# A fused attention and gMLP kernel: another recorded order for four compute engines, and a narrower marking product

## The chip, the cores and the metric

The kernel runs on one core of one Trainium2 chip. A core has five engines that run their own instruction streams in order: TensorE (PE, matrix products), VectorE (DVE), ScalarE (ACT), GpSimd (POOL) and SyncE (SP, which here only issues transfers). [...] The metric is device time in microseconds (us), the median over runs; smaller is better.

## What is computed

The input x has 2048 tokens of 512 numbers, in bf16. A linear attention block with 32 heads and a residual is followed by a gMLP mixer with a residual:

```
def _A_ref(x, wqkv, wo):
    qkv = (x @ wqkv).reshape(B, S, 3, H, Dh)        # H = 32, Dh = 16
    phi = lambda t: where(t > 0, t + 1, exp(t)) + 1e-06
    pq, pk = phi(q), phi(k)
    kv = einsum('bhsd,bhse->bhde', pk, v)
    z = einsum('bhsd->bhd', pk)
    num = einsum('bhqd,bhde->bhqe', pq, kv)
    den = einsum('bhqd,bhd->bhq', pq, z)[..., None] + 1e-06
    return (num / den).transpose(0, 2, 1, 3).reshape(B, S, D) @ wo

def _B_ref(x, w_in, w_sp, b_sp, w_out):
    z = gelu(einsum('bsd,df->bsf', x, w_in))        # F = 1792
    z1 = z[..., :Fh]                                # Fh = 896
    z2 = layernorm(z[..., Fh:])
    g = einsum('ts,bsf->btf', w_sp, z2) + b_sp[None, :, None]
    return einsum('bsf,fd->bsd', z1 * g, w_out)

h = x + _A_ref(layernorm(x), A_wqkv, A_wo)
h2 = h + _B_ref(layernorm(h), B_w_in, B_w_sp, B_b_sp, B_w_out)
```

## The kernel before

**How the order is set.** The kernel does not issue instructions as its code is read. Each step is recorded in a list by `_Prog.add` (an engine, a function that issues the instructions, the memory it reads and writes), and the dependencies are found from the overlap of the footprints: pieces of on-chip memory, and whole banks of the accumulator memory (psum, 8 banks of 512 floats per partition). `schedule` (L144) then decodes the string `ORDER` (L16), a compressed list of the numbers of all 1315 recorded steps in the order in which they are to be issued; each engine gets its own part of it, in that order. `emit` (L163) puts a semaphore wait before each step whose input comes from another engine. The string and the record together fix all five streams: 349 steps on PE, 456 on VectorE, 255 on ACT, 129 on GpSimd and 126 on SP. A step may issue several instructions (eight matmuls, say).

Since an engine runs in order, a step that waits holds up all that stands behind it on its engine. An order can therefore change which engine waits for which, and for how long, without a change of what is computed.

**The stages, in time.**

1. *Head and K stage (0 to 46 us).* `k_unit` (L648) takes the tokens in 16 tiles of 128. VectorE computes the statistics of a tile (L543, L544); `norm` (L588, on VectorE or ACT) writes the normalised tile xn; it is turned round, for the first four tiles by PE (`pe_transposes`, L602), for the others by a transposing transfer on SP (recorded through `dma_t`, L467), into xnT. PE multiplies with the K part of wqkv (all products of the helper `matmuls` show up as L434). `phi` (L609) has ACT write exp into e (all of ACT's work through its helper shows up as L453), VectorE clamp it (L614) and combine it into pk (L617, L619). PE adds pk and xn up into four banks over all tiles (L692). A few of the Q products (`q_unit`, L698) are between these. In the same stretch VectorE forms sums of weights (`comb`, L755, into ws and sae) for the block scheme described below.
2. *Small products and h tiles (46 to 73 us).* Context, wv and wo are folded into one matrix m (L790, L801). Denominators (L824) go through ACT (r, rcp) and are spread over partitions by transfers on SP (`spread`, L815, writes r16; the trace names it r); VectorE multiplies them into pqT (L840). For each of 16 token tiles PE forms pqT × m in one of the banks 4, 5 and 7 in turn, VectorE adds x and writes h (L852, which frees the bank), ACT squares it, GpSimd makes mean and variance of it, VectorE normalises (hn, L588), and SP turns it round into hnT.
3. *First mixer stage (66 to 108 us).* z = gelu(hn × w_in). For pairs of tiles, `cell3` (L905) and `cell2` (L922) use a scheme with 7 block products in place of 8, whose input sums are formed on VectorE (hs, ws) and whose outputs are combined by copies of ACT and additions of VectorE within the banks (`add_on`, L882). ACT applies gelu into z2 or z1. z2 is normalised: VectorE or ACT statistics (L952, L953), GpSimd, VectorE (L588).
4. *Spatial product (104 to 212 us).* `mix` (L1067) forms w_sp × z2 for pairs of row tiles in the same 7-product manner (sums wt, sa, zt on VectorE), some of it nested once more (`nested`, L1042, with nu, nv, np). The gate multiplies with z1 (L1030, L1031), SP turns the result round into zgT.
5. *Output (from 175 us, between the steps of 4).* `mo_pair` (L1159) multiplies zgT with w_out for two tiles, again with 7 block products (us, vs sums on VectorE; tmp reads L1176; h written at L1188), and SP stores h.

**The marking product.** A bank of which only a part has been written by a product gets a product of no use into its rest, before later products accumulate onto parts of it. Before, bank 7 gets a 512-column product that starts anew (L1210); bank 4, used by the last pair, gets one over the rest of the bank, 64 columns from HW = 448 to 512 (L1217). Neither contributes to the output.

Of the kernel before, what the change touches and what calls it, by code (L numbers as in the profile page):

```python
# [32 lines left out]
class _Prog:  # L33
# [219 lines left out]
def bass_sequential_preLN__linear_attn_block__mixer_gmlp__prompt_kernel(  # L253
# [11 lines left out]
    _, S, D = A_x.shape  # L265
    F = B_w_in.shape[1]
    FH = F // 2
    H = 32
# [9 lines left out]
    g = _Prog(nc)  # L278
# [43 lines left out]
    x = g.sbuf("x", o_x, [NT, D], BF16)  # L322
    h = g.sbuf("h", o_x, [NT, D], BF16)
# [6 lines left out]
    hnT = g.sbuf("hnT", o_pk, [KD, S], BF16)  # L330
# [4 lines left out]
    z1 = [g.sbuf(f"z1t{n}", o_xnT + slot[n] * ZR, [FH], BF16) for n in range(NT)]  # L335
# [14 lines left out]
    N4 = HT // 2 * (HW // 2) * 2  # L350
# [65 lines left out]
    def bank(b, n=512, lo=0):  # L416
        return psum[:, b, lo:lo + n]
# [5 lines left out]
    def PE(fn, reads, writes, ns, **k):  # L423
        return g.add("PE", fn, reads, writes, cost=ns, lat=165, **k)
# [372 lines left out]
    for c in range(KD):  # L797
        b = CB[1 - c % 2]
# [18 lines left out]
    for tg in range(NG):  # L817
# [12 lines left out]
        if tg not in MERGE:  # L830
# [135 lines left out]
    lo, hi = slice(0, HW), slice(HW, FH)  # L966
# [227 lines left out]
    for k in range(0, HT, 2):  # L1194
# [5 lines left out]
        if k == 0:  # L1200
# [6 lines left out]
                quarter_sums(nv1, z2[:, 0:HT, lo])  # L1207
            if any(m & 2 for m in NEST):
                quarter_sums(nv5, zt1)
    PE(lambda pe: pe.matmul(bank(7), lhsT=hnT[:, 0, 0:P], rhs=wout[:, 0, :], start=True, stop=True), [hnT[:, 0, 0:P], wout[:, 0, :]],  # L1210
       [bank(7)], 216)
    wout_sums()
    for c, i in enumerate(MIX[:-1]):
        X, Y = (3, 4) if i == MIX[-2] else (6, 7)
        if Y != 7:
            rest, any_, w = psum[:, Y, HW:512], zgT[MIX[0]][:, 0, :], wout[:, 0, 0:512 - HW]
            PE(lambda pe, rest=rest, any_=any_, w=w: pe.matmul(rest, lhsT=any_, rhs=w, start=False, stop=True,  # L1217
                                                               skip_group_check=True), [any_, w], [rest], 65)
        mo_pair(i, c % 2, X, Y)
# [34 lines left out]
```

## Time and profile before

| | before |
|---|---|
| runs | 224.6, 223.45, 224.06 us |
| median | 224.06 us |
| span of the profiled execution (first to last instruction) | 222.3 us |
| median less that span | 1.76 us |
| granted TensorE clock, mean | 1.000 |
| busy: PE, VectorE, ACT, GpSimd | 97%, 91%, 64%, 21% of the span |
| moved by transfers | 27.12 MB, mean 122 GB/s |

The profiled execution is told by its span; no whole time is listed for it. In rows of the timeline the columns are start, duration, engine, line, operation, output <- inputs, shape and count; a bracket at the end is the idle time just before, and what released the engine. Matmuls overlap, so that a row's duration is longer than its share of the time: the distance from the start of one row to the start of the next is what counts. Rows by stage give, after the stretch and its length, the busy time (and count) of PE, PE's weight loads, VectorE, ACT and GpSimd, the granted clock, the share of the transfer engines, and GB/s; a row for one engine has that engine alone. In a group of instructions the last columns are total busy time, mean ns of one, and idle time before them.

### The profile page before, as it was taken

To read this page: it belongs to the slowest core of one execution; us is meant where nothing else is said; L and a number is where in the kernel's file an instruction comes from. 1 tells how busy PE (TensorE), PEld (TensorE's weight loads), DVE (VectorE), ACT (ScalarE), POOL (GpSimd) and SP (SyncE) were. 2 spreads that over 40 slices of the span, in tenths; PEclk is the share of its full clock that TensorE was granted. 3 is DMA by queue.
4 is the path that set the end of the run, shared out by engine and by line. 5 is a ranking of instruction groups with operands and counts; after the bars stand their busy time and mean duration, and the time that the engine had idled before them with its cause. 6 is when DMAs were issued, how large, how long until landed. Compare 5 with 4: busy or idle time off the path is not lost.

```text
span 222.3 us, 3865 instructions
## 1 busy us (share of the span) xinstructions
PE 216.2 (97%) x1346; PEld 123.6 (56%) x1346; DVE 202.8 (91%) x472; ACT 142.8 (64%) x283; POOL 47.1 (21%) x133
## 2 busy tenths in 40 slices
PE   7799999999999999999999999999999999999995
PEld 7443444443344444444555556666676787767764
DVE  3899967899999999999989998999999989899995
ACT  5789663299889999999872546626475246732330
POOL 4334410000547554685720000000000000000000
PEclk9999999999999999999999999999999999999999
DMA  6758877928966555304993653995372205033574
GB/s 182 246 99 227 170 180 181 237 50 193 182 137 132 112 107 85 49 0 94 179 134 88 166 116 81 161 202 107 58 152 58 41 0 70 17 88 27 127 203 142
DMA packets 75026, 27.12 MB, mean 122 GB/s; under 512 B 64768, under 2 KB 75008, under 8 KB 75008
## 3 DMA queue, kind: packets, MB, share of 16 engines
q1 hardware_dynamic: 74304, 26.30, 57.0%
q10 hardware_dynamic: 704, 0.59, 0.9%
q8 instruction: 10, 0.16, 0.3%
q14 instruction: 8, 0.07, 0.1%
HBM read 6.95 MB, written 2.10 MB: 41 GB/s over the span
## 4 chain that ended last, share of the span: by engine, by line
PE 87%; DVE 4%; DMA 3%; ACT 3%; SPq 1%; issue 1%; ACTq 0%
PE psum L434 79%; PE psum L692 6%; DMA x<-in_A_x_dram 1%; SPq L815 1%; DMA r<-rcp 1%; ACT e L453 1%; DVE pqT L840 1%; DVE h L852 1%; DVE st L543 1%; DVE pk L619 1%; PE psum L602 0%; PE psum L824 0%; PE psum L714 0%; PE psum L790 0%; DVE e L614 0%
## 5 line engine op out<-in xcount | busy, mean ns | idle before, releaser
L453 ACT ACTIVATE psum<-psum 128x448 f32<-128x448 f32 (+2 forms) x76 | 31.1, 428 | 34.9 <-PE psum L434 28.6
L434 PE MATMUL psum<-z,wt 128*128 128x448 bf16 (+1 forms) x216 | 42.0, 335 | 0.1
L434 PEld LDWEIGHTS psum<-z,wt 128*128 128x128 bf16 x216 | 20.9, 98 | 14.6 <-ACT np L453 0.4
L434 PE MATMUL psum<-win,hnT 128*128 128x448 bf16 x112 | 26.4, 353 | 0.0
L453 ACT ACTIVATE e<-psum 128x1024 bf16<-128x1024 f32 (+1 forms) x18 | 16.7, 929 | 8.5 <-PE psum L434 8.5
L453 ACT ACTIVATE z1t<-psum 128x448 bf16<-128x448 f32 (+1 forms) x24 | 16.4, 691 | 7.3 <-PE psum L434 5.3
L434 PE MATMUL psum<-ws,hs 128*128 128x448 bf16 x72 | 19.2, 353 | 0.0
L434 PEld LDWEIGHTS psum<-win,hnT 128*128 128x128 bf16 x112 | 10.5, 98 | 11.0 <-ACT z1t L453 1.0
L434 PE MATMUL psum<-zt,sa 128*128 128x448 bf16 (+1 forms) x92 | 16.5, 316 | 0.0
L882 DVE TENSOR_TENSOR psum<-psum,p5z 128x448 f32<-128x448 f32 x24 | 15.0, 626 | 1.0 <-ACT z1t L453 0.8
L692 PE MATMUL psum<-pk,xn 128*128 128x512 bf16 x64 | 15.8, 379 | 0.1
L453 ACT ACTIVATE p<-psum,b 128x448 f32<-128x448 f32 x22 | 13.4, 634 | 3.6 <-DVE u L1030 1.8
L434 PE MATMUL psum<-m,pqT 128*128 128x512 bf16 x64 | 14.7, 380 | 0.9 <-DVE h L852 0.6
L434 PE MATMUL psum<-xnT,wqkv 128*128 128x512 bf16 x64 | 15.3, 379 | 0.0
L453 ACT ACTIVATE z<-psum 128x896 bf16<-128x896 f32 x16 | 15.0, 970 | 0.2 <-PE psum L434 0.2
L434 PE MATMUL psum<-wqkv,xnT 128*128 128x512 bf16 x64 | 15.0, 379 | 0.0
L1030 DVE TENSOR_TENSOR u<-psum,p 128x448 bf16<-128x448 f32 x22 | 13.6, 620 | 1.4 <-PE psum L434 1.0
L434 PE MATMUL psum<-wout,zgT 128*128 128x256 bf16 (+1 forms) x77 | 14.9, 302 | 0.0
L434 PE MATMUL psum<-nv,nu 128*128 128x224 bf16 x108 | 14.5, 259 | 0.1
L543 DVE BATCH_NORM_STATS2 st<-x 128x6 f32<-128x512 bf16 x15 | 9.8, 682 | 3.6 <-DMA x<-in_A_x_dram 3.6
L614 DVE TENSOR_SCALAR e<-e 128x1024 bf16<-128x1024 bf16 (+1 forms) x18 | 7.0, 390 | 5.6 <-ACT e L453 5.6
L434 PEld LDWEIGHTS psum<-zt,sa 128*128 128x128 bf16 x92 | 8.9, 98 | 5.3
(157 smaller groups left out, 452.2 us busy)
## 6 DMA issues: line engine op xcount, KB each, us to landing
r<-rcp SPq DMA_DIRECT2D x16, 128.0 KB, 2.7
out_dram<-h SPq DMA_DIRECT2D x15, 128.0 KB, 1.8
win<-in_B_w_in_dram SPq DMA_DIRECT2D x4, 448.0 KB, 3.8
x<-in_A_x_dram SPq DMA_DIRECT2D x6, 256.0 KB, 3.8
wqkv<-in_A_wqkv_dram SPq DMA_DIRECT2D x2, 512.0 KB, 4.9
wout<-in_B_w_out_dram SPq DMA_DIRECT2D x1, 896.0 KB, 5.1
wt<-in_B_w_sp_dram SPq DMA_TRANSPOSE x32, 4.1
wo<-in_A_wo_dram SPq DMA_DIRECT2D x1, 512.0 KB, 6.4
```

Of the source, the lines that this page charges most:

```text
L434: inst = pe.matmul(out_ap, lhsT=a, rhs=b, start=start and i == 0, stop=stop and i == len(pairs) - 1, **kw)
L453: return g.add("ACT", lambda ac: ac.activation(out_ap, in_ap, func, **kw), [in_ap, *extra], [out_ap] + ([accum] if accum is not None else []),
L543: dve(lambda v: v.bn_stats(s[:, 0:6], src[:, n, :]), [src[:, n, :]], [s[:, 0:6]], D)
L614: dve(lambda v: v.tensor_scalar(e, e, 1.0, EPS_PHI, op0=ALU.min, op1=ALU.add), [e], [e], w * GW, acc=4)
L619: dve(lambda v: v.scalar_tensor_tensor(dst, t, 1.0 + EPS_PHI, e, op0=ALU.add, op1=ALU.max), [t, e], [dst], w * GW, ps=True)
L692: inst = pe.matmul(bank(CB[c]), lhsT=xn[:, i, c * P:(c + 1) * P], rhs=pk[:, i, :], start=i == 0, stop=i == NT - 1)
L815: g.add("SP", lambda q: q.dma_start(dst, src_ap), [rcp[:, i:i + w, :]], [dst], cost=700, lat=2200, dma=f"r{tg}{c // 2}")
L840: dve(lambda v, q=q, r=r: v.tensor_tensor(q, q, r, ALU.mult), [q, r], [q], 2 * GW, acc=2)
L852: dve(lambda v, n=n, b=b, s=s: v.scalar_tensor_tensor(h[:, n, :], bank(b), 1.0, x[:, n, :], op0=ALU.mult, op1=ALU.add, accum_out=s[:, 0:1] ...
L882: dve(lambda v: v.tensor_tensor(half(b), half(src), p, ALU.add), [half(src), p], [half(b)], HW, ps=True)
L1030: dve(lambda v: v.tensor_tensor(u, half(b), p, ALU.add), [half(b), p], [u], HW, ps=True)
```

## The change

The string `ORDER` is replaced. SP's sequence of 126 steps is the same in both. Of the steps that exist in both, 188 of PE's 349 have another place in their engine's sequence, 396 of VectorE's 456, 138 of ACT's 255 and 84 of GpSimd's 129; most move by a few places, 5 on PE, 120 on VectorE, 12 on ACT and 17 on GpSimd by more than 5, and the furthest by 15, 99, 15 and 11.

In the record itself one step goes and one comes: the 512-column marking product of bank 7 is removed, and the first output pair (`c == 0`, banks 6 and 7) gets the 64-column one that only the last pair had. It reads zgT of the first tile and wout; the removed one read hnT and wout.

```
-ORDER = "c-jrsg92EG76ibvyXVHXZM%(a+qN4!jcwbuZQHgR+kEdQX3Qd3M1#e%kQT`z...
+ORDER = "c-jTQ0{|EY5Cp)zz5Up>8{4+i#<p#{v28WBZQHhO+v!Y101;q_hmdd(kr4@D...
...
-    PE(lambda pe: pe.matmul(bank(7), lhsT=hnT[:, 0, 0:P], rhs=wout[:, 0, :], start=True, stop=True), [hnT[:, 0, 0:P], wout[:, 0, :]],
-       [bank(7)], 216)
     wout_sums()
     for c, i in enumerate(MIX[:-1]):
         X, Y = (3, 4) if i == MIX[-2] else (6, 7)
-        if Y != 7:
+        if c == 0 or Y != 7:
             rest, any_, w = psum[:, Y, HW:512], zgT[MIX[0]][:, 0, :], wout[:, 0, 0:512 - HW]
             PE(lambda pe, rest=rest, any_=any_, w=w: pe.matmul(rest, lhsT=any_, rhs=w, start=False, stop=True,
                                                                skip_group_check=True), [any_, w], [rest], 65)
```

Moves that the prediction speaks of: on ACT xn15 is written before xn14; on VectorE an h eviction (L852) goes ahead of an e clamp (L614) and another eviction; three sums of w_sp rows (L755, wt and sa) go 99, 86 and 60 places back, and a sum of w_in's weights 68 places back; on PE two products win,hnT go 14 places ahead, among the h tiles.

More of the change, by code (lines that the diff above doesn't have):

```diff
@@ new lines @@
+ORDER = "c-jTQ0{|EY5Cp)zz5Up>8{4+i#<p#{v28WBZQHhO+v!Y101;q_hmdd(kr4@DAq0quC<uoTh>K{5k0gkW1jvO%NQgX0jHJkoyhw?BNQPAS3;9t1$&ng`kpcx#1ceX-p^zSF5E?}h6SWZrX%P!GQ4Hx&2ept9ZIA(Vks0-n39V2ZSrHyt&=##x0@;uQ?a&aV&>q>*2=!40<<SBC&=C#L1^rP0f1@Nip)_*hA5=tN#6}hTi_WNo0jP?BsEo4ciovLci5P??7>^-{gX(CEVVHpHn1mXbjB=QQ;b@A5=!R*SikWDJq3Dk0n2uTKfyHQnC0K->Xo;nmfo150kywtKSb^PGi4oX|)mVkz*oDU!h5xVzd$9)lFdBU@1_y8hv#}q~F&1+$4u>%p>o5-ou@;B$1Y7Y8>v05IumSV25nF5<7T_svVLOiDA$H&>9$^!X<19|#DqdnUuHhu^;S4U~9Nys+E@6kA$7#I4WrVN`_=rykX`gWg9}v?*87-EXg|;vj+rGdpo+YyQ_7#yWvB~0CVBe6$eju(zv90zU$?YdnSycPW6522PL0C&_u;>=e!dWs)V83x6sV#=(v6Pm^idtR^Z|UtHOJQj(pB1z67SYmKev4oQEQ6J`+E&ntTOo^NcTvI$TV^Y1b*!G1vLcqnN?QeMYgsL$RkWN|-&$EY%VasMu2r(u*3&9m8LMJ#tey3->{it_TQ%!t+3b)Fx4!nb9k!Y_${N^f)Uw>x-Wu95Yh+(7mo>J3t%>cl(bn5K*fi^C)oqM*vJtk#npzE;ZX<1`b+)C}#cpGUEw@?L&z4z#`)2!Wfc<C9Y`+b(yVl&k+X@?GN9?$Dx1%=OZrec{YdvhG{j?J{&hFTFYhfpCj&-$r_P_?)T<d11?1vq&RW`vM+C;l=L+zJ6vX=H1tL>sawt4o-F4=s`#vwMvPTOl+W0x&Euh?%pW5aBcowfM<V>x)v-q<2rYvNT~XWQ(pkqay*ui1HXzOw|3%c&NU#(-ch#^WnIvB{Q*p%{XRnVX@x&=N8a!|=K#;d{Gbk$KbBTWTidM%!TB7=>Y(k5T!-(y%)h+Xaipa4f{U49~QDYCRa85m<oFEI;co9iQ7Ri^xsZi!oS`wV0lTS(LRIlRcS%u~?TMtr%ZeGS+8C7GWR8W&;*yZ<gg>?8{7S$d^`vnOTqh*phLWoQ=4R<(Pt>>|d5=E2iXjR$wG%VQcQ-9DcTeOvN_r&x+i|tQ^3({EtI8h;6x(vssBHIiEv0n3cJo?YNu6Sc+A+fa6$|!#R&%>^-+zX)a`AmSKCYWHol+A-+LJ-oYY{XA_R#-(1BBe1OGl%D0@zkzCDx*o>oijGefKqq)l_u{oFUILB};5AYrL+EPyD2QK3YF6UT&<P`4VI!@(hPU9!8;9(x*dbZ#O?&BA3<aB=JCLZB;?y;l%#<Tpv&iu(4{Ka!Lug>4R$64IWF8sr-JVW>v(%-|qnqOex^7FjQ5I&Qq8PY?0D6h%1evx6k2E+O(hVx6j%9FgzJABA14DXTrKCdx?@3u#Lz=&SMBYRg~XB3a-j~Uf(@Cl>)Q&#dAUd3a1On=5gev`4iw%=kLkL#8FHtTvkf6jy+-)s6y?qx1d;JH1KzhFL3>`6U|=l6R4ip4yc7xxDKn)UrJFX3;P!t;1?Z|EgGrI+$_p4tn0X|Lr)J)<}BGG4?}c{wlOjs0&g@5jB4XY-2Q#M}8l-rUQ2dvD<xytP_;UT@_cyp5WAXYZseUeG6d4{xWAp2?eeC$H`mJiWK{em>pXdKX{fReiXYc?S*f72egm`3zs{{e7T!_bEQjXL=hy?5jPe&+_#?*w^?5@9F>fCZFnAeYUUi-ag0E_)72PM|_Bn_d&kS7x+*=;UhG{H~KK|<KKO_pY*=I(6{(e-|Qp(U!Utge6%0)dH&NEdk&xPTYZ!t@(I4k$M{m;>8E^~FZTm}+PC{bf8skloObyckD%Xv)_40O|Knr*u}2a#&iD94-|LZe&a?Y9kE)Bl&!fu~Md$sxXZC2i<QF`KOt<}t@An)2+$VWVbyOF%6?MliyOdHd{FjH<O~311l}fSn)I%xIRe$O2b<b~kH^tE_kF6f+uF&eG``%eSHBa&M%zG=YMrow})dP>O{tBV_>Z6A~Pzf|heU(@VHCjpZ+WRS)255|iD6HOiBK@VITBxxar->S`q<ZTUlvW`%N$)(JQfRWOD3_*cfu?JUwkeD<XuFbYn$l>7QmdfSYnEnew&p04cIvZd)FSQBVtw)VzC=}(Sxa?J%d|oT^ud?wys~JeK6-XVRB3(kHOi`W%Ar-ttuk7z!K$W0%BH;9sEf*}4O*)U%A@t#rF`10%_^+Fm0w%5M_aX52eeQB=&M&(5$)GEuc3n~tC~8ZqN=51dZyYsr01%uayqO!I;rwHp`)s&mpZOXI-|=vt>U_(YbvIzdZ9)tp&J^e`f99FDyi#gpbBcLn`)+pYOY(Vs5`o?dupOes;o_Vpu2jg`w9`X&?CLlYyBq%7PM5zV6L7hPViWvf>!e2jlu+>gLeuSoRWgD!CQUMSp`A(;JqRRPxVnzf(Svh;EUo05ra?qrs%<EMGoQxKNL0is-KDx#1CQxF@s<Ft^`4%Aa?Lu34=dM93V&%{0|2SilG"
@@ L1209, in bass_sequential_preLN__linear_attn_block__mixer_gmlp__prompt_kernel @@
                 quarter_sums(nv5, zt1)
-    PE(lambda pe: pe.matmul(bank(7), lhsT=hnT[:, 0, 0:P], rhs=wout[:, 0, :], start=True, stop=True), [hnT[:, 0, 0:P], wout[:, 0, :]],
-       [bank(7)], 216)
     wout_sums()
@@ L1214, in bass_sequential_preLN__linear_attn_block__mixer_gmlp__prompt_kernel @@
         X, Y = (3, 4) if i == MIX[-2] else (6, 7)
-        if Y != 7:
+        if c == 0 or Y != 7:
             rest, any_, w = psum[:, Y, HW:512], zgT[MIX[0]][:, 0, :], wout[:, 0, 0:512 - HW]
```

1 line of the change is left out of this document (removed).

## The prediction

> **What bounds the kernel now.** I read the page's first part, then the chain of waits, then the timeline of PE around the places where the chain leaves PE, then the busy time by stage of the engine named there.
>
> ```profile
> PE 216.2 (97%) x1346; PEld 123.6 (56%) x1346; DVE 202.8 (91%) x472; ACT 142.8 (64%) x283; POOL 47.1 (21%) x133
> PE 87%; DVE 4%; DMA 3%; ACT 3%; SPq 1%; issue 1%; ACTq 0%
> 64.11 2.80 DMA r<-rcp
> 67.68 29.59 PE psum L434 x152
> 176.12 0.21 PE psum L1210
> 212.07 0.03 PE psum L1217
> ```
>
> TensorE sets the end: it is busy for 97% of the span, and from 67.68 us the chain stays on it almost without a break. No product of the computation is added or taken away, so an order can only move the time in which PE stands still. Busy shares hide these, because matmuls overlap; the start of one row and the start of the next show them:
>
> ```profile
> 58.39 1.04 PE L434 MATMUL psum<-m,pqT 128*128 128x512 bf16 x4 [0.37 <-DVE h L852]
> ...
> 62.70 3.63 PE L434 MATMUL psum<-m,pqT 128*128 128x512 bf16 x16 [0.25 <-DVE h L852]
> 66.16 1.30 PE L434 MATMUL psum<-win,hnT 128*128 128x448 bf16 x6
> 67.68 3.63 PE L434 MATMUL psum<-m,pqT 128*128 128x512 bf16 x16 [0.23 <-DVE pqT L840]
> ...
> 71.52 0.92 PE L434 MATMUL psum<-win,hnT 128*128 128x448 bf16 x4
> 72.28 0.54 PE L434 MATMUL psum<-ws,hs 128*128 128x448 bf16 x2
> ...
> 75.73 0.92 PE L434 MATMUL psum<-win,hnT 128*128 128x448 bf16 x4
> ```
>
> Sixteen products of 512 columns take 62.70 to 66.16, 0.216 each; four of 448 take 71.52 to 72.28, 0.19 each. Against these paces the middle of the kernel stands still at:
>
> ```profile
> 96.73 0.54 PE L434 MATMUL psum<-ws,hs 128*128 128x448 bf16 x2
> 97.32 0.93 PE L434 MATMUL psum<-win,hnT 128*128 128x448 bf16 x4
> ...
> 103.11 0.92 PE L434 MATMUL psum<-ws,hs 128*128 128x448 bf16 x4
> 103.99 0.55 PE L434 MATMUL psum<-ws,hnT 128*128 128x448 bf16 x2
> ...
> 136.99 0.55 PE L434 MATMUL psum<-zt,sa 128*128 128x224 bf16 x4
> 137.66 0.56 PE L434 MATMUL psum<-z,wt 128*128 128x224 bf16 x4
> ```
>
> Two products from 96.73 should end at 97.11 and the next start at 97.32: 0.21 lost. In the same way 0.88 from 103.11 for four (0.76) loses 0.12: 0.33 in these two, and four smaller holes between 83 and 99 us have some 0.2 together. At 136.99 four products of 224 columns, half as wide, should take 0.38 and take 0.67: 0.29 lost. Whatever an order can win here lies in these holes and in the three bracketed waits, 0.85 in all.
>
> **The change part by part, on the time of before.** I laid the new order of each engine beside the old one and gave each instruction the duration of its row.
>
> *Head and K stage, 0 to 51 us: 0.* VectorE runs one more statistics op before the first exp's clamp, the transposes on PE are split by the first projection, GpSimd's memsets move later. PE then waits for the same things. ACT normalises xn15 before xn14, while SP's queue still issues the transpose of 14 first, so 14 waits about two ACT ops longer and everything behind it on SP goes with it: transpose 15, the bias, half of win1, two transposes of a w_sp row, wv and wo.
>
> ```profile
> 30.29 0.80 ACT L453 ACTIVATE xn<-x,rs 128x512 bf16<-128x512 bf16 x1
> ...
> 29.52 2.78 SPq L467 DMA_TRANSPOSE xnT<-xn  x2
> ...
> 37.22 0.58 SPq L464 DMA_DIRECT2D wqkv<-in_A_wqkv_dram  x1
> ...
> 47.95 1.06 PE L790 MATMUL psum<-ct,wqkv 128*128 128x128 bf16 x16
> DMA to landing us min/median/max: 4.6/5.2/5.4
> ```
>
> The transpose that started at 29.52 would start when the ACT op of 30.29 and one more (0.80) are through, near 31.9: 2.4 late. That moves the issue of wv from 37.22 to 39.6, and with at most 5.4 to land it is there at 45.0, 2.9 before its product at 47.95. The cover is that 2.9; if the landing were as late again, PE would wait some 2. I take 0; bounds −0.1 (the head's own hole) and +0.4.
>
> *The h tiles, 51 to 76 us: −0.54.*
>
> ```profile
> 56.69 0.42 DVE L614 TENSOR_SCALAR e<-e 128x1024 bf16<-128x1024 bf16 x1
> ...
> 57.63 0.69 DVE L852 SCALAR_TENSOR_TENSOR h<-psum,x 128x512 bf16<-128x512 f32 x1
> ```
>
> The eviction of 57.63 frees the bank for which PE waits 0.37 at 58.39. In the new order it stands ahead of the clamp of 56.69 and of the eviction between the two rows, 57.63 − 56.69 = 0.94 of VectorE's work, so this wait goes. The last one, 0.23 at 67.68, is for the reciprocals that SP spreads (the chain's 64.11 DMA); VectorE's product still waits for it, but PE's queue now holds work for the gap: the two win,hnT products of 75.73 stand ahead of the last h tiles, 2 × 0.19 = 0.38 of work that is later not there. Since the stall is followed by h tiles which start as VectorE frees their banks, part of the 0.38 only shifts the wait. Walking the two orders to the h tile at 67.68 I find PE 0.16 ahead of before, and 0.54 ahead once the 0.38 is counted. Bounds: 0 (each gap reopens one bank later) and −0.85 (0.37 + 0.25 + 0.23).
>
> *First mixer stage, 76 to 108 us: −0.3.*
>
> ```profile
> 70.00:80.00 10.00, 10.00 (x54) 4.80 (x52) 9.99 (x28) 9.29 (x21) 6.29 (x19) 1.00 0.56 110
> ...
> 90.00:100.00 10.00, 9.96 (x53) 4.68 (x51) 9.98 (x23) 10.00 (x21) 7.62 (x15) 1.00 0.17 26
> ...
> PEld psum L434 <- DVE psum L882: 2.4, 9, 0.4
> ...
> 45.31 0.62 DVE L755 TENSOR_TENSOR ws<-win,ws 128x896 bf16<-128x896 bf16 x1
> ...
> 72.85 0.68 DVE L755 TENSOR_TENSOR wt<-wt,wt 128x1024 bf16<-128x1024 bf16 x1
> ...
> 86.74 0.64 DVE L755 TENSOR_TENSOR sa<-wt 128x1024 bf16<-128x1024 bf16 x1
> ```
>
> Three engines are full here (columns: PE, weight loads, VectorE, ACT, GpSimd), and the wait of PE's loads that recurs is for VectorE's additions into banks (L882). The new order takes sums for the spatial product out of this stretch: those of 72.85 and 86.74 go 99 and 86 places back, to where the span is past 115 us, and a third like them 60 places; the sum of the win1 weights of 45.31 comes in from the K stage. That is, at 0.6 from start to start, 3 × 0.6 − 0.6 = 1.2 less of VectorE's work ahead of the additions. It exceeds the holes, so I let the 0.33 close but for 0.03, and count nothing for the small ones, since ACT, at 10.00 of 10.00, feeds some of these banks. Bounds 0 and −0.55 (0.33 and the 0.2).
>
> [...] The rows of one form in a stretch with GpSimd and in one without it differ by 2 ns:
>
> ```profile
> L755 DVE TENSOR_TENSOR wt<-wt,wt 128x1024 bf16<-128x1024 bf16 x2 | 1.4, 681 | 0.0
> ...
> L755 DVE TENSOR_TENSOR wt<-wt,wt 128x1024 bf16<-128x1024 bf16 x5 | 3.4, 683 | 0.0
> ```
>
> [...]
>
> *108 to 140 us: 0.* The hole at 137 is a chain of ACT and VectorE work whose order does not change on any of the three engines; 0 to −0.1.
>
> *The marking product: −0.18.* The chain shows the 512-column one at 176.12 with 0.21 and the 64-column one at 212.07 with 0.03. It stays in the same place and its operands are long there.
>
> *Mixer's second half, 140 to 205 us: +0.2.*
>
> ```profile
> 145.00:150.00 5.00, 4.50 (x11) 1.00 1.01 192
> 150.00:155.00 5.00, 4.57 (x12) 1.00 0.61 123
> ...
> 180.00:185.00 5.00, 4.16 (x13) 1.00 0.01 2
> ...
> 190.00:195.00 5.00, 4.01 (x12) 1.00 0.00 0
> ...
> 176.81 0.75 DVE L1176 TENSOR_TENSOR tmp<-psum,h 128x256 f32<-128x256 f32 x2
> 178.07 0.49 PE L434 MATMUL psum<-wout,zgT 128*128 128x256 bf16 x3
> ```
>
> VectorE prepares sums for the products to come and evicts their results. The new order puts 1.07 to 1.40 more of sums ahead of the two tmp reads of 176.81, whose bank PE's product of 178.07 overwrites. From 177.56 to 178.07 there is 0.51 of slack, and VectorE's idle time of 145 to 155 (0.50 + 0.43) can take up the rest, 0.89. But idle time is only of use for sums whose inputs are there. Bounds 0 and +0.89; I take +0.2, nearer to covered, as 0.93 of idle is just more than is needed.
>
> *Sum:* 0 − 0.54 − 0.3 + 0 − 0.18 + 0.2 = −0.82. The profiled execution's span of 222.3 becomes 221.5. The median of the runs lies 224.06 − 222.3 = 1.76 above that span, so 223.2.
>
> **The rivals.**
>
> *All holes close (chance 0.24).* Every term at its low bound: −0.1 − 0.85 − 0.55 − 0.1 − 0.18 = −1.78, 222.3. For it: VectorE is relieved in both early stretches by more than the holes there. Against: a bank that comes free earlier only helps as long as the next one does too.
>
> *Given back (0.16).* PE gets ahead by 76 us, and waits for ACT in 80 to 100, where ACT shows no idle time; 0.71 of idle in 70 to 80 is all that ACT can bring forward, and it may not lie behind inputs that come earlier. What is left is the −0.18: 223.9, and with the +0.2 of the second half 224.1.
>
> *VectorE becomes the bound after 140 us (0.18; slower).* The added sums find no idle time: 0.89 at 178; and ahead of the later pair's tmp reads, which the idle stretch of 190 to 195 precedes, the new order puts 2.58 more of work, of which the idle of 180 to 185 and 190 to 195 (0.84 + 0.99) covers 1.83 or nothing. That is 0.89 + 0.75 = 1.64 at least and 3.47 at most; with the −1.02 of the other terms +0.6 to +2.5, so 224.7 to 226.5, in the middle 225.6. It decides from 178 us. Against: laid on the times of before, PE is not yet waiting for those later reads.
>
> *The SP queue is late (0.05; slower).* wv lands after 47.95 by as much as a second landing would be late: +2 − 0.82, 225.2.
>
> **How the numbers follow.** The forecast, 223.2, has 0.31, its own range 222.5 to 223.9. A measurement of this kernel can tell 0.5% (1.1 us) from no change: faster is below 222.9, slower above 225.2. Of the forecast 0.12 lies below 222.9, of the first rival 0.23: faster 0.35. Slower: 0.15 of the third rival, 0.04 of the fourth, and 0.06 for a cover that fails elsewhere among some hundreds of moved instructions: 0.25. The rest, 0.40, is within 0.5%. The range reaches from below the first rival's 222.3 to the middle of the third: 222.0 to 225.6.
>
> **What would show it.** In the timeline of PE after: no bracket at the second group of h tiles and a win,hnT row among them; starts at 0.19 pace around 96 to 104; the same 0.29 hole near 136; a row of 0.03 in place of the 0.21; at the tmp reads near 176 no wait of PE for VectorE. PE's waits for VectorE after 140 us in sum over 0.5 would make the prediction wrong on the slow side; a wait for ACT near 80 to 100 that is longer than before would be the second rival.

## The result and the profile after

| | before | after |
|---|---|---|
| runs side by side | 223.45 to 224.6 us (4) | 225.6 to 226.52 us (4) |
| median | 223.94 us | 226.34 us |
| ratio after / before, 95% interval | | 1.0097 [1.0069, 1.0125] |
| span of the profiled execution | 222.3 us | 223.9 us |

The changed kernel is slower by 1.0%, where 0.4% faster was forecast, and above the range's end of 225.6. The profiled execution of after, at 225.6 us, is the fastest of its four. A second profile of the same kernel, taken later (e18 below, span 224.8), stands nearer to the median, and both are read here.

The first part and the chain of waits of the page of after:

```profile
PE 216.8 (97%) x1334; PEld 123.8 (55%) x1346; DVE 203.1 (91%) x472; ACT 142.9 (64%) x283; POOL 48.0 (21%) x133
PE 61%; DVE 14%; ACT 11%; DMA 5%; POOL 3%; issue 2%; SPq 1%; POOLq 0%; DVEq 0%; ACTq 0%
```

Twelve matmul records of 1346 are missing from the first count. The busy shares are those of before. What changed is the chain: PE's share of it falls from 87% to 61%, and VectorE and ACT go from 7% to 25%. PE now waits at more places, for work that waited itself.

To see where, I laid the start of each product of after against the same product in the profile of before; the differences are PE's lateness. Its growth by stretch:

| stretch | forecast | after | after, second profile |
|---|---|---|---|
| up to 47 us | 0 | +1.05 | +1.15 |
| 47 to 77 (h tiles) | −0.54 | −0.36 | −0.35 |
| 77 to 101 | −0.3 | −0.22 | −0.22 |
| 101 to 122 | 0 | +0.52 | +0.82 |
| 122 to 138 | 0 | +0.05 | +0.08 |
| 138 to the last product | −0.18 + 0.2 | +0.41 | +0.95 |

The forecast's own stages end at 51, 76, 108 and 140 us, so that 0.12 of the −0.3, the hole at 104, belongs to the row after it. The holes that the forecast looked at did close, nearly as far as it said for this one pair of profiles, and the time was lost at places that it had put at 0.

**The first loss, up to 47 us.** The timeline of after on ACT, SP's queue, VectorE and PE, in this order:

```profile
29.98 1.02 ACT L453 ACTIVATE e<-psum 128x1024 bf16<-128x1024 f32 x1 [2.30 <-PE psum L434]
30.89 1.51 ACT L453 ACTIVATE xn<-x,rs 128x512 bf16<-128x512 bf16 x2
...
28.63 0.58 SPq L464 DMA_DIRECT2D win<-in_B_w_in_dram  x1
32.43 2.50 SPq L467 DMA_TRANSPOSE xnT<-xn  x2
...
43.20 0.69 DVE L755 TENSOR_TENSOR sae<-wt 128x1024 bf16<-128x1024 bf16 x1 [1.44 <-DMA wt<-in_B_w_sp_dram]
...
46.61 0.27 DVE L721 TENSOR_TENSOR zc<-zT,selm 128x128 bf16<-128x128 f32 x1
...
46.93 0.40 PE L824 MATMUL psum<-pqT,zc 128*32 128x512 bf16 x4 [0.37 <-DVE zc L721]
```

Both normalisations, xn15 and xn14, stand behind an exp that waits 2.30 us for PE. SP's queue asks for xn14 first, and so it issues nothing from 29.21 to 32.43; before, this pair of transposes went out at 29.52. All that follows in the queue up to 42 us is 2.6 to 3.4 us late, the transposes of a w_sp row too (36.86 and 41.83 in place of 34.24 and 38.39). VectorE needs that row for the sum sae, which the new order has put ahead of the chain that ends in zc (before, it stood behind zc). The sum waits 1.44 us, zc goes with it, and PE waits for zc.

**The h tiles and the first mixer stage.** VectorE, then PE:

```profile
60.31 0.41 DVE L588 TENSOR_SCALAR hn<-h,st,rs 128x512 bf16<-128x512 bf16 x1 [0.46 <-POOL rs L583]
...
55.33 4.48 PE L434 MATMUL psum<-m,pqT 128*128 128x512 bf16 x20
...
63.82 1.90 PE L434 MATMUL psum<-m,pqT 128*128 128x512 bf16 x8 [0.53 <-DVE pqT L840]
65.56 0.54 PE L434 MATMUL psum<-win,hnT 128*128 128x448 bf16 x2
...
96.37 0.92 PE L434 MATMUL psum<-win,hnT 128*128 128x448 bf16 x4
97.13 0.54 PE L434 MATMUL psum<-ws,hnT 128*128 128x448 bf16 x2
97.51 0.92 PE L434 MATMUL psum<-ws,hs 128*128 128x448 bf16 x4
```

The waits of 0.37 and 0.25 for an eviction are gone, 20 products (five h tiles) run in one row without a bracket, and two win,hnT products stand among the tiles. But a wait of 0.53 for VectorE's product with the reciprocals is new at 63.82: that product stands behind an hn which waits 0.46 us for GpSimd. From 96.37 on four products take 0.76 and two 0.38, the pace, where before 0.21 was lost before 97.32.

**The second loss, 101 to 122 us.** PE in after, and the same place in its second profile:

```profile
110.40 1.68 PE L434 MATMUL psum<-z,wt 128*128 128x448 bf16 x8
112.31 0.55 PE L434 MATMUL psum<-win,hs 128*128 128x448 bf16 x2 [0.23 <-DVE psum L882]
112.69 0.54 PE L434 MATMUL psum<-ws,hs 128*128 128x448 bf16 x2
113.31 1.69 PE L434 MATMUL psum<-z,wt 128*128 128x448 bf16 x8
```

```profile
110.51 1.68 PE L434 MATMUL psum<-z,wt 128*128 128x448 bf16 x8
112.72 0.55 PE L434 MATMUL psum<-win,hs 128*128 128x448 bf16 x2 [0.53 <-DVE psum L882]
```

Eight products should take 1.52; the next start comes after 1.91 and 2.21. So 0.39 and 0.69 are lost to an addition of VectorE into a bank (L882), and 0.24 more after 112.69 (two products, 0.38; 0.23 in the second profile), where the next row needs the last normalised z2.

**The third loss, from 138 us.** In the second profile, ACT, then PE:

```profile
141.77 0.54 ACT L453 ACTIVATE z1t<-psum 128x448 bf16<-128x448 f32 x1 [0.82 <-DMA zgT<-z1t]
...
142.37 0.56 PE L434 MATMUL psum<-z,wt 128*128 128x224 bf16 x4 [0.39 <-ACT z1t L453]
```

A gelu of ACT writes a buffer from which SP's queue still reads an earlier tile (the transpose into zgT); PE waits 0.39 for it. The first profile of after does not have this wait. The other hole of that stage is unchanged, and the narrow marking product does what was said:

```profile
138.04 0.55 PE L434 MATMUL psum<-zt,sa 128*128 128x224 bf16 x4
138.71 0.56 PE L434 MATMUL psum<-z,wt 128*128 128x224 bf16 x4
...
177.52 0.20 PE L1215 MATMUL psum<-wout,zgT 128*128 128x64 bf16 x1
177.55 1.68 PE L434 MATMUL psum<-zt,wt 128*128 128x448 bf16 x8
```

0.67 for four products of 0.38 as before, 0.29 lost; and 0.03 from the marking product to the next start, where the wide one took 0.21.

### The profile page after: what moved, and what is told of

Same layout as the page of the kernel before. It is cut to its first block, busy times and chain, and to the rows that moved or that the text cites. A ratio compares the mean times of both kernels' runs of the same rounds, so it can differ in the third digit from the quotient of the medians.

```text
span 223.9 us, 3851 instructions
## 1 busy us (share of the span) xinstructions
PE 216.8 (97%) x1334; PEld 123.8 (55%) x1346; DVE 203.1 (91%) x472; ACT 142.9 (64%) x283; POOL 48.0 (21%) x133
## 4 chain that ended last, share of the span: by engine, by line
PE 61%; DVE 14%; ACT 11%; DMA 5%; POOL 3%; issue 2%; SPq 1%; POOLq 0%; DVEq 0%; ACTq 0%
PE psum L434 56%; PE psum L692 5%; DMA x<-in_A_x_dram 3%; ACT z L453 3%; DVE st L543 2%; DVE st L952 2%; ACT z1t L453 2%; DVE z L588 2%; DMA zgT<-z1t 1%; ACT sq L453 1%; DMA r<-rcp 1%; POOL rs L551 1%; DVE pk L619 1%; DVE pqT L619 1%; ACT e L453 1%
## 5 line engine op out<-in xcount | busy, mean ns | idle before, releaser
L434 PE MATMUL psum<-ws,hs 128*128 128x448 bf16 x72 | 18.7, 353 | 0.0
L882 DVE TENSOR_TENSOR psum<-psum,p5z 128x448 f32<-128x448 f32 x24 | 14.8, 625 | 0.2 <-PE psum L434 0.2
L434 PE MATMUL psum<-wout,zgT 128*128 128x256 bf16 (+1 forms) x71 | 12.5, 296 | 0.0
L567 POOL TENSOR_SCALAR st<-st 128x1 f32<-128x1 f32 x10 | 3.3, 334 | 39.5 <-ACT sh L453 32.4
```

The source lines that it names most:

```text
L434: inst = pe.matmul(out_ap, lhsT=a, rhs=b, start=start and i == 0, stop=stop and i == len(pairs) - 1, **kw)
L567: pool(lambda p: p.tensor_scalar(s[:, 2:3], s[:, 0:1], s[:, 0:1], -1.0 / (n * n), op0=ALU.mult, op1=ALU.mult), [s[:, 0:1]], [s[:, 2:3]], 240)
L882: dve(lambda v: v.tensor_tensor(half(b), half(src), p, ALU.add), [half(src), p], [half(b)], HW, ps=True)
```

## The experiments

Every kernel here has the narrow marking product; what differs is the order of each engine. A cut at a time means that each engine follows one of the two orders up to what it starts by then, and the other from there on, with steps that fall out of it put at the cut. SP's sequence is one and the same in all. Ratios are to the kernel before, with 95% intervals, 0.001 being 0.22 us.

**The marking product alone.**

```
 ORDER: that of before
-bank 7: product of 512 columns (L1210)
+bank 7: product of 64 columns
```

> The order of before on all engines, with only the marking product changed (64 columns, in the place of the 512-column one). Theory: PE is 0.18 us shorter and nothing else moves: 0.1 to 0.3 us faster than before. Rival: the narrower product has to wait for the first zgT, and a part of the loss comes from here: slower by 0.2 or more.

0.9995 [0.9983, 1.0008], 224.04 against 224.28 us, span 221.9. The product goes from 175.75 to the next start at 175.78, 0.03 as in after; in the time the predicted 0.18 is 0.1, within the interval.

**Where the loss arises: cuts.**

```
+ORDER: changed up to 23 us (e2), 48 (e3), 104 (e5), 140 (e4), then that of before
+ORDER: that of before up to 48 us, then changed (e6)
+ORDER: that of before up to 140 us, then changed (e16)
```

> The new order up to 23 us on every engine, the order of before from there on, the narrow marking product. Theory: the new head makes VectorE wait for a load of x and puts a statistics operation ahead of the evictions, and PE starts the products after 22 us some 0.6 us late: 0.3 to 0.6 us slower than before with the 0.2 of the marking product off. Rival (all of the loss lies after 140 us, where VectorE becomes the bound): as fast as before, or 0.2 faster.

> The new order up to 48 us on every engine, then the steps that are left in the order of before. Theory: the head's 0.6 and another 0.5, since VectorE waits for a late w_sp transfer ahead of zc, and PE for zc: 0.7 to 1.1 us slower than before; PE shows a wait of about 0.5 at the denominator product near 46 us. Rival: as cut at 23 us.

> The new order up to 140 us, where all engines have the same set of steps behind them in both orders, then the order of before. Theory: 0.9 to 1.2 us slower than before in the span, and 0.3 to 0.5 faster than the changed kernel. Rival (VectorE becomes the bound after 140 us): within 0.3 of before, so that nearly all of the changed kernel's loss goes.

> The new order up to 104 us, the steps that are left in the order of before. The cut at 48 us cost 0.4 us and the cut at 140 us 2.0, so 1.5 lie between. Theory: 0.6 of them is the mix of win1 and spatial products at 110 to 113 us, where PE waits for an addition into a bank and for the last z2, and 0.9 is front lateness that the new h tiles no longer absorb: 0.8 to 1.4 slower than before, and no wait of over 0.1 of PE at 110 to 113. Rival (all of the 1.5 lies in the h tiles and the first mixer stage): 1.8 to 2.2 slower.

> The other way round: the order of before up to 48 us, the new one from there on. Theory (the late front is what the rest cannot absorb): the new h tiles gain 0.2, the first stage 0.2, the marking product 0.2, against 0.3 to 0.6 lost at 110 us and 0.3 in the second half: within 0.4 of before. Rival (the stages after 48 us lose by themselves): 1.2 us slower or more.

> The order of before up to 140 us, the new one from there on, with the narrow marking product. Theory: the second half alone loses 0.3 to 0.6 (PE waits for VectorE's gates and h evictions near 177, 182 and 213 us), 0.2 of it covered by the marking product: 0.1 to 0.5 slower than before. Rival (it only loses behind the new middle): 0 to 0.2 faster than before.

| kernel | ratio | median, us | span, us |
|---|---|---|---|
| e2, new to 23 | 0.9999 [0.9981, 1.0017] | 224.52 | 222.8 |
| e3, new to 48 | 1.0022 [1.0004, 1.004] | 224.7 | 223.0 |
| e5, new to 104 | 1.0125 [1.0103, 1.0146] | 227.06 | 225.3 |
| e4, new to 140 | 1.0084 [1.0063, 1.0105] | 226.26 | 224.4 |
| e6, new from 48 | 1.0062 [1.004, 1.0084] | 225.74 | 224.0 |
| e16, new from 140 | 1.002 [1.0003, 1.0037] | 224.7 | 223.0 |

The differences give the loss by stretch: e2 less e1 +0.1 us; e3 less e2 +0.5; e4 less e3 +1.4; from 140 us +0.3 (after less e4) to +0.55 (e16 less e1). Each step has an uncertainty of 0.5 to 0.6, so that only the stretch from 48 to 140 stands well clear by itself. It costs more in the times than in the two profiles (0 and +0.33 from 47 to 138): in e3 PE is 1.67 late at 47.6 and 0.88 at 68.6, and in e1 it is 0.42 late at 58.8 and 0.19 early at 67.5. The old h tiles take lateness up too.

The profile of before is one execution, and the same reckoning against it can be done for every kernel here. The growth of PE's lateness, in us (at each end of a stretch the median over the products that start within 1.2 us of it in before):

| stretch | old order there | new order there |
|---|---|---|
| 24 to 47 us | 0 in all seven (e1, e2, e6, e12, e15, e16, e17) | +0.43 to +1.03 in nine, median 0.66; 0 in the three with xn14 ahead of the exp (e7, e11, e14, below) |
| 47 to 77 | 0 to −0.78, median −0.43 (e1, e2, e3, e16, e17) | −0.23 to −0.47, median −0.36 (twelve) |
| 77 to 122 | 0 to −0.02 (the same five) | +0.30 to +0.98, median 0.60 (the same twelve) |
| 138 to the last product | −0.17 to −0.19 (e1, e2, e3, e5, e12, e15, e17) | +0.38 to +0.40 in seven; more with the wait near 142 us |

From 122 to 138 it grows by 0 to 0.08, but for e6 (0.25) and e17 (1.10, below). The medians of old and new differ by 0.66, 0.07, 0.62, 0.06 and 0.56, about 2.0 of the 2.3 us between e1 and the mean of after's two measurements; the wait near 142 us, in some executions, is not in it. At 24 us old and new do not differ clearly: the six kernels with the old head are 0.3 to 1.0 later than before's own profile there, the others 0.2 to 0.8 but for e3 (1.2) and e9 (1.6). So of the 1.05 of after up to 47 us, 0.62 was there at 24, and only the rest, 0.43, can be put to the moves behind that point.

e5 is a poor cut. Three sums that the changed order has deferred fall at 104 us all at once, and the additions behind them come late. PE there:

```profile
105.90 0.54 PE L434 MATMUL psum<-ws,hs 128*128 128x448 bf16 x2
107.07 0.55 PE L434 MATMUL psum<-ws,hnT 128*128 128x448 bf16 x2 [0.63 <-DVE psum L882]
...
109.73 0.54 PE L434 MATMUL psum<-ws,hs 128*128 128x448 bf16 x2
111.74 0.55 PE L434 MATMUL psum<-ws,hs 128*128 128x448 bf16 x2 [1.46 <-DVE psum L882]
```

0.79 and 1.63 are lost, 2.4 in place of the 1.8 that three sums of 0.6 hold. It measures what sums cost at that place, and not the stretch up to 104.

**The first loss: xn14 ahead of the exp.**

```
-ACT: e (waits for PE), xn15, xn14
+ACT: xn14, e (waits for PE), xn15
```

> The changed kernel with one step of ACT moved back: xn14 is written before the exp that waits for PE near 30 us, as before, so that SP's queue can issue its transpose. Theory: SP no longer stands 3 us, the first w_sp transfers land 2 to 3 us earlier, VectorE's wait of 1.4 us at 42 us goes, zc is there in time, PE's wait of 0.5 near 46 us goes: 0.3 to 0.6 faster than the changed kernel (ratio to before 1.007 in place of 1.0097). Rival (a zc that is 0.5 earlier is swallowed by the waits for the reciprocals at 58 to 64 us): no change in time, though the wait near 46 us is gone.

1.0061 [1.0041, 1.0081], 225.89 us. SP's queue, VectorE and PE:

```profile
29.48 3.01 SPq L467 DMA_TRANSPOSE xnT<-xn  x2
...
34.43 3.09 SPq L467 DMA_TRANSPOSE wt<-in_B_w_sp_dram  x2
...
41.25 0.68 DVE L755 TENSOR_TENSOR sae<-wt 128x1024 bf16<-128x1024 bf16 x1
...
45.45 0.27 DVE L721 TENSOR_TENSOR zc<-zT,selm 128x128 bf16<-128x128 f32 x1
...
46.07 0.40 PE L824 MATMUL psum<-pqT,zc 128*32 128x512 bf16 x4
```

The queue runs on at 29.48, the sum finds its row, and PE starts on zc without a wait at 46.07 in place of 46.93; of these 0.86, about 0.4 is from earlier in the head, where the two executions already differed. Against the mean of the two measurements of after (1.0098) the ratio falls by 0.0037, 0.8 us, give or take 0.6. This mechanism is shown, by e7 and by the first row of the table above; e6, which leaves the same stage as it was before, gains as much.

**The wait near 112 us: the addition moved ahead.**

```
-VectorE: two z2 normalisations, addition (L882), ..., sum, addition (L882)
+VectorE: addition (L882), two z2 normalisations, ..., addition (L882), sum
```

> The changed kernel with two of VectorE's additions into banks moved ahead: the first one of the z1 cell near 111 us ahead of two normalisations of z2, the second ahead of a sum of w_sp rows. Theory: PE's wait of 0.4 to 0.7 near 111 us goes, the wait for the last z2 at 113 us grows by no more than 0.2: 0.3 to 0.5 faster than the changed kernel. Rival (VectorE is the bound there and any order of the same work ends at the same time): the wait only moves to the last z2, no change.

1.0122 [1.0098, 1.0146], 227.24 us. PE:

```profile
110.62 1.68 PE L434 MATMUL psum<-z,wt 128*128 128x448 bf16 x8
112.14 0.54 PE L434 MATMUL psum<-win,hs 128*128 128x448 bf16 x2
112.51 0.54 PE L434 MATMUL psum<-ws,hs 128*128 128x448 bf16 x2
114.19 1.69 PE L434 MATMUL psum<-z,wt 128*128 128x448 bf16 x8 [1.14 <-DVE z L588]
```

The wait for the addition is gone, and the one for z2 grows from 0.23 to 1.30: a second piece of VectorE's work takes the place of the first.

**One or two sums of w_sp moved behind.**

```
+VectorE: the sum that the changed order has at 104 us goes behind the last z2 normalisation, 113 us (e10)
+VectorE: this sum, and the one before the second addition, go behind that addition (e13)
```

> The changed kernel with one sum of w_sp rows (0.6 us of VectorE) moved from 104 us to behind the last normalisation of z2 at 113 us; its first user comes at 121 us. Theory (VectorE is the bound from 100 to 114 us): PE's waits near 111 and 113 us, 0.6 to 0.9 together, shrink by 0.4 to 0.6, and the kernel is that much faster than the changed one (ratio to before 1.007 to 1.008). Rival (the additions wait for ACT's copies, not for VectorE's turn): the waits stay, no change.

> The changed kernel with two sums of w_sp rows (1.2 us of VectorE in all) moved from 104 and 113 us to behind the second addition of the z1 cell near 114 us. Theory (VectorE, busy without a break from 56 to 116 us, sets the time at which PE gets its inputs at 111 to 115 us): the four waits there, 0.6 to 0.9 together, shrink to 0.1 to 0.3, and the kernel is 0.4 to 0.7 faster than the changed one (ratio to before 1.007 to 1.008). Rival (the sum moved alone did nothing, since the waits are for ACT's chain): no change.

e10: 1.0103 [1.0086, 1.0121], 226.67 us; the waits of 0.39 and 0.24 become four of 0.18 to 0.23. e13: 1.0124 [1.0099, 1.0149], 227.17 us. PE in e13:

```profile
110.56 1.68 PE L434 MATMUL psum<-z,wt 128*128 128x448 bf16 x8
112.16 0.55 PE L434 MATMUL psum<-win,hs 128*128 128x448 bf16 x2
...
116.95 0.54 PE L434 MATMUL psum<-ws,hs 128*128 128x448 bf16 x2
117.89 1.69 PE L434 MATMUL psum<-zt,sae 128*128 128x448 bf16 x8 [0.40 <-DVE zt L755]
```

Of the 0.39 before the addition's product 0.08 is left (112.16), but 0.56 is lost before 117.89. Three ways to reorder VectorE's work here moved the stall and left its sum or more; the loss is not in the place of any one of these steps. Of the eight places by which the first addition had moved back on VectorE (107.62 us before, 111.63 in after), e8 undid three.

**The wait near 142 us.**

```
-ACT: gelu of tile 15, copy u of tile 8
+ACT: copy u of tile 8, gelu of tile 15
```

> The changed kernel with one step of ACT moved back: the u of tile 8's gate is written before the gelu that waits 1.7 us for PE near 130 us, as before. Theory: the gate of tile 8 is done 2 us earlier, SP issues its transpose and the w_sp transfer behind it 2 us earlier, and the transpose of tile 9 has the transfer engines to itself, so that ACT's write into tile 9's buffer near 140 us never waits for it (it waited 0.7 and 1.1 us in the cut at 140 us and in the run with the additions moved): the gate's transpose is issued near 130.5 instead of 132.5, time 0 to 0.5 faster than the changed kernel. Rival (the two late landings are chance): transpose earlier, no change in time.

1.0123 [1.0107, 1.014], 227.03 us. The edit did not reach its aim: the transpose of tile 8 into zgT was issued at 133.69, later than the 132.54 of after, since VectorE's gate for it stands behind an addition that waits for the same gelu; PE is 1.1 us later in this execution, so that against PE the issue did not move. Where the wait of 0.82 comes from was not settled by it.

**Repairs together.**

```
+e11: xn14 as in e7, copy u as in e9, sum as in e10; order of before from 140 us
+e12: order of before up to 48 us and from 140; between, changed, with the copy u and the sum moved
+e14: the two sums as in e13, xn14 as in e7; order of before from 140 us
```

> The changed kernel with the three moves together (xn14 and tile 8's u on ACT moved back, the w_sp sum behind the last z2) and the order of before from 140 us on. Theory: -0.6 to -0.8 (xn14), -0.5 (sum), 0 to -0.4 (u), -0.4 (second half): 1.5 to 2.1 faster than the changed kernel, within 0.4 of before. Rival (the front's gain is swallowed later as it was in before): 0.8 faster than the changed kernel.

> The order of before up to 48 us and from 140 us on, the new one between, with tile 8's u and the w_sp sum moved as above, and the narrow marking product. Theory: the new middle keeps its gains of 0.3 at the h tiles and 0.3 in the first mixer stage, and loses 0 to 0.3 at 111 us: 0.2 to 0.7 faster than before. Rival (the new middle loses by itself, as in the kernel with the order of before up to 48 us): 0.5 to 1.2 slower than before.

> The same two sums, xn14 before the waiting exp on ACT, and the order of before from 140 us on. Theory: all three losses off, front, backlog at 111 us and second half: 0.2 to 0.6 slower than before, the rest being the head. Rival: as the run with three moves (0.9 slower).

e11: 1.0041 [1.0023, 1.0059], 225.25 us. e12: 1.0038 [1.0022, 1.0054], 225.2 us. e14: 1.0045 [1.0028, 1.0061], 225.12 us. All three take back a little over half of the loss, and about 1 us over e1 is left. In e12 only the middle is new, and it leaves as much as the others.

**The good moves alone.** The gains that the forecast counted on, put into the order of before:

```
+VectorE: h eviction (57.63) ahead of the e clamp (56.69) and the eviction between
+PE: the two win,hnT products ahead, among the h tiles
```

> The order of before with the narrow marking product and two of the new moves alone: the h eviction ahead of an e clamp and another eviction on VectorE, and the win2,hnT product of 75.7 us moved on PE into its wait near 67.5 us. Theory (VectorE is the bound from 56 to 116 us): PE's holes at 58 and 67 us close, 0.4 to 0.8, but PE waits as much more for VectorE before 116 us: within 0.2 of the order of before with the narrow marking product. Rival (the prediction's sum: PE is the bound, and a filled hole stays won): 0.5 faster than before, or more.

1.0019 [1.0007, 1.0031], 224.71 us, slower than e1. PE:

```profile
55.80 3.72 PE L434 MATMUL psum<-m,pqT 128*128 128x512 bf16 x16
60.03 0.40 PE L824 MATMUL psum<-pqT,zc 128*32 128x512 bf16 x4 [0.51 <-DVE pqT L617]
...
78.32 0.92 PE L434 MATMUL psum<-win,hnT 128*128 128x448 bf16 x4
79.29 0.55 PE L434 MATMUL psum<-ws,hnT 128*128 128x448 bf16 x2
```

Sixteen products, four h tiles, run without a wait, and then PE stands for 0.77 (60.03 − 55.80, less 16 × 0.216) until VectorE has formed the pqT that the moved eviction pushed back; 0.21 more goes before 79.29.

```
+order of before, VectorE: three sums of w_sp from 72.9, 86.7 and 119.5 us to 122, 128 and 130
```

> The order of before with the narrow marking product, and three sums of w_sp rows (0.6 us of VectorE each) moved: those of 72.9 and 86.7 us to 122 and 128 us, the one of 119.5 us to 130 us. Nothing else moves. Theory (VectorE is the bound from 56 to 122 us, so less of its work there helps, where filled holes of PE did not): PE is 0.3 to 0.8 earlier at 104 us, some of it lost at 122 to 132 us; 0.1 to 0.6 faster than before. Rival (PE is the bound there): no change beyond the 0.1 of the marking product.

1.005 [1.0031, 1.0069], 225.14 us. PE:

```profile
97.24 0.54 PE L434 MATMUL psum<-ws,hs 128*128 128x448 bf16 x2
97.82 0.93 PE L434 MATMUL psum<-win,hnT 128*128 128x448 bf16 x4
...
130.22 1.68 PE L434 MATMUL psum<-z,wt 128*128 128x448 bf16 x8
132.82 0.55 PE L434 MATMUL psum<-ws,hnT 128*128 128x448 bf16 x2 [0.93 <-DVE psum L882]
```

The hole of 0.20 at 97.82 is the one of before to 0.01: less of VectorE's work in 72 to 104 did not close it, though VectorE now stands idle there for 1.04 us, against 0.04 in e1. The hole at 104 stayed too (0.13). And behind the moved sums PE loses 1.08 before 132.82 (2.60 less eight products of 0.19), waiting for an addition.

**The changed kernel again.**

> The changed kernel itself, once more, beside the others: ratio to before 1.0097 (1.007 to 1.0125) the first time; the runs with one part edited without effect gave 1.010 to 1.012. Theory: 1.009 to 1.012, and a profile like one of theirs, with PE some 2 us later than before at its end rather than 1.45.

1.0099 [1.0072, 1.0125], 226.66 us, span 224.8: the result stands, and the waits at 47, 112 and 142 of this execution are larger than in the first (1.67 in place of 1.44 for the sum sae).

None of the versions beats the kernel before by more than its interval; e1, the marking product alone, is level with it.

## Why the prediction was wrong

**The head and K stage, put at 0, cost 0.6 to 0.8 us** (e3 less e1; after less e7). This is the first step that failed. The delay itself was foreseen, as were its size (2.4 us; it was 32.43 − 29.52 = 2.9) and the list of what stands behind it on SP. The cover was then tested for one user alone, PE's product with wv. The w_sp row on the same list has its user on VectorE, and the new order had moved that user from behind zc to ahead of it. With this, the fourth rival was right about the queue and wrong about the transfer; at 0.05 it was priced too low. e7 shows it.

**The h tiles, −0.54, gave −0.36 in the profile and no time.** The two eviction waits went as worked out. But the old order takes up as much lateness in this stretch, 0 to 0.78 us, as the new one does, 0.23 to 0.47, so that against it nothing was won. The bound "each gap reopens one bank later" was near the truth: the reciprocals' product became late, and alone in the old order the moves cost 0.5 us (e15 less e1: 0.0024, give or take 0.0017, which is 0.4).

**The first mixer stage, −0.3, and 108 to 140 us, 0: the second step that failed.** From 48 to 140 us the forecast, h tiles and all, had −0.84, and the times have +1.4. Three things were wrong in it. The holes at 97 and 104 were ascribed to VectorE's load, because the recurring wait of the weight loads is for it; e17 takes the load away and the holes stay. For the larger one the profile of before names another engine, a gelu of ACT, and an addition of VectorE only for the smaller:

```profile
97.31 0.49 PEld L434 LDWEIGHTS psum<-win,hnT 128*128 128x128 bf16 x4 [0.48 <-ACT z1t L453]
...
103.99 0.11 PEld L434 LDWEIGHTS psum<-ws,hnT 128*128 128x128 bf16 x2 [0.41 <-DVE psum L882]
```

In the new order the products of 97.32 stand five places later on PE, at 100.16, and that hole is gone, which PE's order can explain and the moved sums cannot. The count of "1.2 less of VectorE's work ahead of the additions" went by where the steps had been and not by where the additions of each order stand: of the three deferred sums, the one of 60 places comes at 104.16, ahead of the additions that PE needs at 112, and a sum that the new order has brought forward, from 118.40 to 113.16, stands ahead of the second of them. And the bounds, 0 and −0.55, allowed for no loss, though the quoted rows showed VectorE at 9.98 of 10.00. Over 56 to 116 us VectorE's busy time is 58.38 before and 58.75 after, and the waits of PE's weight loads for its additions (in the whole span: total us, count, longest) show where it went:

```profile
PEld psum L434 <- DVE psum L882: 2.7, 9, 0.7
```

In all 2.7 for 2.4, but the longest is 0.7 in place of 0.4. What e8, e10 and e13 show is that the wait moves and does not go, whichever of these steps of VectorE is moved. The traces show what has come together there: on PE three rows of eight products (zt,sae at 103.97, z,wt at 108.13 and 110.40) now stand ahead of products of a z1 cell that they followed before, the cell's second product starts at 109.64 in place of 106.28, and its two additions come at 111.63 and 113.77 in place of 107.62 and 110.08, among the last normalisations of z2, which PE needs near 113.3 in both orders. That this order of PE is the cause is argued and not shown, since PE's order of that stretch was not put back by itself.

The second rival, "given back", had the place wrong (a wait for ACT in 80 to 100) and the kind of thing right: PE made up 0.58 of lateness between 47 and 101 us (1.05 to 0.47) and lost 0.52 in the next 20.

**The second half, +0.2, cost 0.3 to 0.55.** The mechanism was right and the size off: the term was taken "nearer to covered" within 0 and 0.89, and the truth was in the middle (0.38 + 0.18 = 0.56 in the profiles). The sign that the prediction named came: after 141 us PE's weight loads wait seven times for VectorE, 1.7 us in all, in after and in e16, against twice and 0.36 us before. Most of it is covered. At the tmp reads themselves they wait 0.16 and PE loses 0.04; more goes at other results of VectorE, as before 181.44 in e16 (PE, then its weight loads):

```profile
180.90 0.55 PE L434 MATMUL psum<-zt,sa 128*128 128x224 bf16 x4
181.44 0.50 PE L434 MATMUL psum<-wout,zgT 128*128 128x256 bf16 x3
...
181.44 0.22 PEld L434 LDWEIGHTS psum<-wout,zgT 128*128 128x128 bf16 x3 [0.25 <-DVE h L1188]
```

0.54 for four products of 0.38. The third rival's 1.64 did not come, though its time, 225.6, is the nearest of all to what was measured: that is luck, since most of the loss lies before 140 us.

**The marking product, −0.18**, and the unchanged hole of 0.29 were right.

**The wait at 142 us** was in no part. It occurs in five of the twelve profiles with the new order between 48 and 140 us (e4, e8, e11, e14, e18), and in none with the old one there; the first profile of after is among the seven that do not have it. With the new order tile 8's transpose is issued at 132.54, where it was 130.26 before; a w_sp transpose stands behind it in the queue, and tile 9's after that. Whether the w_sp transfer then holds up tile 9's landing stays open: the one edit meant to tell had no effect on the issue.

The runs also show a fault in the sum's base. Before's own profile, with 222.3, was an early one up to 24 us: with the same order there PE in e1 is 0.33 and in e17 0.97 later than there. Lateness against a single execution is uncertain by that much until the h tiles have taken it up. The three bracketed waits, 0.85 in all, were of that execution too: of e1, e2, e3, e16 and e17, which have the old order there, all show the first (0.36 to 0.56), but the second stands in e17 alone and the third in e2 and e16 alone.

## What to carry to other kernels

When a step is delayed on a transfer queue, follow every transfer behind it to its user in the new order, on all engines: the one that cost here was the one whose user had been moved forward at the same time (VectorE stood 1.44 us for it, ahead of the sum sae). On a stretch where the second engine has hardly any idle time (VectorE in before, busy for 58.38 of the 60 us from 56 to 116), count a moved step as a loss until shown otherwise: in e15 the eviction was moved ahead, its wait went, and PE stood 0.77 us for the result that this had pushed back. Before a hole is put down to an engine's load, look up the wait at that very row: the engine that leads the list of waits need not be the one that is waited for there (VectorE's additions lead it in before, with 2.4 us in all, and the wait of 0.48 at 97.31 was for ACT). And take the holes that are to be closed from more than one execution.

## What the runs showed beside this

One normalisation of 0.8 us behind one waiting exp cost the kernel about as much as itself (0.8 us, give or take 0.6), through four engines: ACT held SP's queue, the queue held VectorE's sum, the sum held zc, and zc held PE. At the links on ACT and VectorE nothing that stood behind the waiting step ran in its idle time (2.30 and 1.44 us in after); in e7, where xn14 stands ahead of the exp, the pair of transposes starts at 29.48 in place of 32.43.

In e5 three sums, 1.8 us, came in front of two waits of PE that lost 2.4, more than their time; whether they account for all of it was not tested.
